# Token-wise softmax and logits turned by VectorE, and w1's split parts ordered behind h's

## The chip, the cores and the metric

The kernel runs on one core of one Trainium2 chip. The metric is device time of one execution in microseconds (us); the kernel before has 1101.79 us as the median of three runs (1101.53 to 1102.30). PE is the matrix engine, DVE the vector engine, ACT the scalar engine, POOL the general engine, SP the engine that issues most DMAs.

## What is computed

An attention over 8 batches with 32 state rows, then a dense expert over its 4608 tokens, then eight experts of which each token takes one:

```python
scores = scale * x @ state.T;   a  = softmax(scores)      # over the states
xread  = a @ state
scores2 = scale * state @ x.T;  a2 = softmax(scores2)     # over the 512 tokens
sread  = a2 @ x
x = concat([xread, sread], axis=2)                        # to 4608 rows of 512
h = x @ w_in;  x = (h * clip(h + 3, 0, 6) / 6) @ w_out
e_idx = argmax(x @ w_gate)                                # one expert for each token
h = maximum(x[mask] @ w1[e], 0);  ye = h @ w2[e]
out[mask] = gate_w * eom * ye
```

All matrices are float32. The large products are made of three: an operand is split into a high part and the rest, and high by high, low by high and high by low are added up.

## The kernel before

**Stages.** Each batch of 512 tokens is one segment of `segs`; two halves of batch 0 frame batch 1, batches 2 to 7 follow, and a last segment holds the 256 state rows. A segment goes through 16 f tiles of the dense expert. For each, `h_xread` makes h with six matmuls of 512 columns (L470), `act` makes g and its parts on ACT and DVE (L499 to L502: r, g, gh, gl), and `gemm2` adds twelve matmuls into four banks (L509 to L511), two tiles later (`LAG` is 2). At some f tiles work of other kinds is slipped in: `timetable` holds, by a step number, the attention of the next batch and the routing of the last one. The Tile scheduler orders each engine's instructions from this; each engine then works through its own list in order. A dependence of the kind `LATER` sets an order on one engine, or between two, and nothing else.

**The softmax over tokens.** `columns` leaves two tiles e (one for each half of the heads), 128 rows of head and state by 512 tokens, with their sums. For the read the tokens must lie on partitions: `cols_turn` (L361) transposes e in eight blocks on PE (L378), and ACT copies them from PSUM as `a2T` (L374). `cols_read` (L384) makes the read in 32 matmuls of 64 columns in four groups of partitions (L393), and ACT scales it by 1/sum (L399). `cols_x1` (L408) turns the 128x128 result with one more PE transpose (L421), which DVE splits as x1h and x1l (L418, L419). `x_loads` and `q_loads` fetch xT and xq, the batch's x in two layouts, through SP; the buffers of the next batch come free with the scores (L226) and the read (L393).

**Routing.** `routed` (L532) takes the dense output out of PSUM into the banks x2. `logits` (L564) makes four matmuls of 512 columns, one for each 128 features, into four groups of 32 partitions (L570). ACT copies the result as l (L575), `turn_logits` (L582) turns it on PE (L591), and DVE adds the four parts into `lg` (L588). `choose`, `ranks`, `place`, `sort_rows` and `scatter` work out each token's place. `write_rows` (L552) turns the rows with DVE (xr, L556) and has SP store them (xd, L562).

**Expert slots.** From about 690 us on 16 slots follow, each of up to 256 tokens of one expert by 8 f tiles, and some pairs. `gemm1` (L1028) makes the parts wh on ACT and wl on DVE of the f tile's w1 (L1034), 12 matmuls of 256 columns into h (L1038), the parts vh and vl of w2 (L1043, L1044), and takes h out of its bank as hh on ACT (L1047) and hl on DVE (L1048). `gemm2e` (L1053) comes two tiles later, `finish` scales the output (y, L1073), `turn` brings the next slot's rows (xt, L953; xh, xl, L973, L974).

Of the kernel before, what the change touches and what calls it, by code (L numbers as in the profile page):

```python
# [8 lines left out]
F32 = mybir.dt.float32  # L9
# [3 lines left out]
AF = mybir.ActivationFunctionType  # L13
# [33 lines left out]
def cat_consts():  # L47

    import numpy as np

    p = np.arange(128)[:, None]
    rows = {
        "desc": np.tile(np.arange(NE, 0, -1), 4),
        "base": np.arange(NE) * CAP,
        "eidx": np.tile(np.arange(NE), 2),
        "k256": np.arange(1, 18) * 256,
        "k256h": np.arange(18) * 256 + 129,
        "k64": np.arange(LEFT // 64 + 1) * 64,

        "pos1": np.array([s // 2 + (s % 2) * (N1 - N1 // 2) for s in range(N1)]),  # L60
        "posm": np.array([s // 2 + (s % 2) * (NM - NM // 2) for s in range(NM)]),
        "posu": np.arange(NU),
    }
    parts = {k: np.tile(np.asarray(a, np.float32), (128, 1)) for k, a in rows.items()}
    parts["half"] = p // 64
    parts["part64"] = p % 64
    parts["tri"] = p < np.arange(128)[None, :]
    off, n = {}, 0
    for k, a in parts.items():
        off[k] = (n, a.shape[1])  # L70
        n += a.shape[1]
    tok = np.zeros((128, NT // 128, 2), np.uint32)
    tok[:, :, 0] = np.arange(NT).reshape(-1, 128).T
    fill = np.zeros((NTAB, 2), np.uint32)
    fill[:, 0] = NT + np.arange(NTAB) % 128
    return off, np.concatenate(list(parts.values()), axis=1).astype(np.float32), tok, fill
# [3 lines left out]
def tile_kernel(  # L80
# [104 lines left out]
    def misc():  # L185
        users.append([])
        return psum("misc", 2), users[-1]
# [173 lines left out]
    def cols_turn(b):  # L361
# [19 lines left out]

        return part

    def cols_read(b):  # L384

        def part():
            a2, r2, copies = e2_t[b]
            x_q = [loads.pop((b, k, "q")) for k in range(2)]
            psR, done = misc()

            def mm(e, i, j):
                h = 2 * j + e
                return T.matmul(psR[32 * j:32 * j + 32, HD * e:HD * e + HD], a2[e][:, i, 32 * j:32 * j + 32],  # L393
                                x_q[h // 4][:, i, HD * (h % 4):HD * (h % 4) + HD], start=(i == 0), stop=(i == 3),
                                tile_position=(0, 32 * j))

            def use():
                for e in range(2):
                    done.append(S.activation(a2[0][:, 0, HD * e:HD * e + HD], psR[:, HD * e:HD * e + HD], AF.Copy,  # L399
                                             scale=r2[:, e:e + 1]).ins)  # L400
                e2_t[b] = a2[0][:, 0, :], list(done)

            return [lambda e=e, i=i, j=j: mm(e, i, j) for e in range(2) for i in range(4) for j in range(4)], \
                [*copies, *q_in[b]], use

        return part

    def cols_x1(b):  # L408

        def part():  # L410
            read, reads = e2_t.pop(b)
            psX, done = misc()
            psX = psX[:, :128]

            def use():
                hi, lo = [x[:, :, NS * b:NS * b + NS] for x in (x1h, x1l)]
                src = psX.rearrange("p (j s) -> p j s", j=4)
                done.append(V.tensor_copy(hi, src).ins)  # L418
                done.append(V.tensor_tensor(lo, src, hi.bitcast(F32), op=ALU.subtract).ins)  # L419

            return [lambda: T.transpose(psX, read, ident)], reads, use  # L421

        return part

    def attn_cols(b):

        if b < 2:
            columns(b, e2_t[b][0])
            yield
        one_run(cols_turn(b))  # L430
        yield
        one_run(cols_read(b))
        yield
        one_run(cols_x1(b))
        yield

    SW = {}
# [114 lines left out]
    def write_rows(r, c):  # L552

        xr = mp.tile([128, 8, 128], F32, tag="xr", name="xr", bufs=2)
        for k in range(4):
            i = V.transpose(xr[:, :, 32 * k:32 * k + 32], r.x2[k][:, 256 * c:256 * c + 256])  # L556
            for d in r.made[1::2]:
                tc.add_manual_dep(i.ins, d.name, LATER, reason="banks first")
        r0 = 128 * r.tile0 + 256 * c
        rows = xd[r0:r0 + 256, :].rearrange("(a u) (g n) -> g u a n", u=32, g=4)  # L560
        for g in range(4):
            D.dma_start(rows[g], xr[32 * g:32 * g + 32])  # L562

    def logits(r):  # L564

        def part():
            psl, done = misc()

            def mm(k):
                return T.matmul(psl[32 * k:32 * k + 32, :r.n], wg_sb[:, k, :], r.x2[k], start=True, stop=True,  # L570
                                tile_position=(0, 32 * k))

            def use():
                r.l4 = mp.tile([128, 512], F32, tag="r", name="l4")[:, :r.n]
                done.append(S.copy(r.l4, psl[:, :r.n]).ins)  # L575
                r.l4_made = done[-1]

            return [lambda k=k: mm(k) for k in range(4)], list(r.made), use

        return part  # L580

    def turn_logits(r):  # L582

        def part():
            pst, done = misc()

            def use():
                done.append(V.tensor_reduce(r.lg, pst[:, :r.n].rearrange("p (t k c) -> p t c k", t=r.nt, k=4),  # L588
                                            axis=AX.X, op=ALU.add).ins)

            return [lambda t=t: T.transpose(pst[:, 128 * t:128 * t + 128], r.l4[:, 128 * t:128 * t + 128], ident)  # L591
                    for t in range(r.nt)], [r.l4_made], use

        return part

# [100 lines left out]
    def route(r):  # L696

        at_will(logits(r))
        write_rows(r, 0)
        yield  # L700
        at_will(turn_logits(r))
        if r.n > 256:
            write_rows(r, 1)
        read_rows(r, 0)
        if r.n > 256:
            read_rows(r, 1)
        yield
        choose(r)
        ranks(r)
        yield  # L710
        place(r)
        sort_rows(r, 0, r.nt)
        if r.n > 256:
            return
        yield
        yield
        scatter(r, last_w[:1])
        yield
        yield
        zero_tails(0, 2)  # L720
        yield
        zero_tails(2, 4)
        yield
# [219 lines left out]
                apart(i, sooner, later_rows)  # L943
        return own

    got_first, last_turned, last_w = [], [], []

    def turn(xg, n):

# [78 lines left out]
    def gemm1(i, ft, xh, xl):  # L1028
# [3 lines left out]
        wh = mp.tile([128, 4, 128], R32, tag="gh", name="wh", bufs=3)  # L1032
        wl = mp.tile([128, 4, 128], R32, tag="gl", name="wl", bufs=3)
        last_w[:] = [S.copy(wh, a).ins, V.tensor_tensor(wl, a, wh.bitcast(F32), op=ALU.subtract).ins]  # L1034
        m = 0
        for w, x in ((wh, xh), (wh, xl), (wl, xh)):
            for k in range(4):
# [6 lines left out]
        V.tensor_tensor(vl, c, vh.bitcast(F32), op=ALU.subtract)  # L1044
        hh = qa["p"].tile([128, 256], R32, tag="hh", name="hh", bufs=3)
        hl = qa["p"].tile([128, 256], R32, tag="hl", name="hl", bufs=3)
        S.activation(hh, ps, AF.Relu)  # L1047
        i = V.scalar_tensor_tensor(hl, ps, 0.0, hh.bitcast(F32), op0=ALU.max, op1=ALU.subtract)  # L1048
        if ft == 6:
            tc.add_manual_dep(i.ins, last_turned[0].name, LATER, reason="the next rows first")  # L1050
        return ft, vh, vl, hh, hl
# [39 lines left out]
    def go(g, n=1):  # L1091
        return lambda: [next(g) for _ in range(n)]
# [72 lines left out]
    def X(b):  # L1165
# [12 lines left out]
        (1, 1): [I(9), go(cols[0]), lambda: q_loads(0)],  # L1178
        (1, 2): [I(10), go(cols[0])],
        (1, 3): [I(11), go(cols[0])],  # L1180
        (1, 4): [go(cols[0]), more_start, I(12)],
        (1, 5): [O(8), I(13)],
        (1, 6): [I(14), O(9)],
        (1, 7): [I(15), O(10)],
# [4 lines left out]
        (1, 12): [O(15), lambda: q_loads(1)],  # L1189
        (1, 13): [go(cols[1]), split_first],  # L1190
        (1, 14): [go(cols[1])],
        (1, 15): [go(cols[1], 2)],
        (0, 8): [load_part],
    }

# [4 lines left out]
    def timetable(b, r, att, shift):  # L1200
# [11 lines left out]
        for k in range(4, 10):  # L1212
            at(k, lambda: next(rows, None))
        if att:
            at(6, lambda: one_run(cols_turn(b)))
            at(7, lambda: one_run(cols_read(b), logits(r)))
            at(8, lambda: one_run(cols_x1(b), turn_logits(r)))
        else:
            at(6, lambda: one_run(logits(r)))
            at(7, lambda: one_run(turn_logits(r)))  # L1220
        at(9, lambda: choose(r))
        at(10, lambda: ranks(r))
        at(11, lambda: place(r), lambda: sort_rows(r, 0, 2))
# [4 lines left out]
    def half_timetable(b, r):  # L1228

        rows = attn_rows(b)  # L1230
        row = lambda: next(rows, None)
        return {
            2: [lambda: write_rows(r, 0)],
            3: [lambda: write_rows(r, 1), row],
            4: [lambda: one_run(logits(r)), row],
            5: [lambda: one_run(turn_logits(r)), lambda: choose(r), row, lambda: read_rows(r, 0), lambda: read_rows(r, 1)],
            6: [lambda: ranks(r), lambda: place(r), lambda: one_run(cols_turn(b)), row],
            7: [lambda: sort_rows(r, 0, 2), lambda: one_run(cols_read(b)), row, row, lambda: one_run(cols_x1(b))],
        }

    for n, (b, f0, f1) in enumerate(segs[:-1]):
# [221 lines left out]
```

## Time and profile before

| | before |
|---|---|
| median of three runs | 1101.79 us (1101.53 to 1102.30) |
| profiled execution | 1100.96 us, its span 1099.2 us |
| granted clock, mean | 0.999 of 2.4 GHz |
| PE busy | 1073.2 us (98%) |
| DVE busy | 714.5 us (65%) |
| ACT busy | 553.7 us (50%) |
| POOL busy | 126.2 us (11%) |
| DMA, mean rate | 134 GB/s |

The profiled execution is one of the kernel's executions, taken with a trace; the span is the time between its first and last recorded work. Busy is the union of an engine's instructions. Matmuls are pipelined, so that their records overlap, and where one begins says more than how long it is. A row with xN groups N like instructions that follow each other; its time runs from the first's start to the last's end.

### The profile page before, as it was taken

The page shows a single profiled execution, that of the slowest core. Times are in us where ns is not written, and L with a number is a line of the kernel's source. Part 1 is how long each engine was busy: PE and PEld are TensorE (multiplying, and loading weights), DVE is VectorE, ACT ScalarE, POOL GpSimd, SP SyncE. Part 2 cuts the span into 40 slices and gives each one's busy share as a digit, 9 for nine tenths or more (in the row PEclk, how much of TensorE's full clock was granted, in tenths as well). Part 3 has the DMA queues.
Part 4 walks back from the last instruction along what each step waited for, and adds up shares of the span by engine and source line. Part 5 has one row for each costly group of instructions (what it writes and reads, how often), then busy time and mean ns, then how long its engine had stood idle before and what let it go on. Part 6 is the DMA issues. An engine that isn't in the chain of part 4 may idle for free. (4 is left out here: it accounts for less than half of the span.)

```text
span 1099.2 us, 18698 instructions
## 1 busy us (share of the span) xinstructions
PE 1073.2 (98%) x6748; PEld 845.6 (77%) x6748; DVE 714.5 (65%) x1518; ACT 553.7 (50%) x1058; POOL 126.2 (11%) x138
## 2 busy tenths in 40 slices
PE   4999999999999999999999999999999999999997
PEld 1577777777777777777777899888869887988994
DVE  7988676755746747556554486986646655667761
ACT  4979644433433434334333344565545654566651
POOL 0000001230030030110300311220010010001001
PEclk9999999999999999999999999999999999999999
DMA  7657043613214114211130159676486679922500
GB/s 252 213 168 248 16 138 96 172 45 77 78 41 116 41 39 116 70 36 53 39 77 1 39 148 288 131 255 231 148 305 186 240 230 334 340 64 64 177 21 31
DMA packets 81251, 147.38 MB, mean 134 GB/s; under 512 B 13232, under 2 KB 49840, under 8 KB 81136
## 3 DMA queue, kind: packets, MB, share of 16 engines
q1 hardware_dynamic: 71776, 118.03, 34.7%
q0 software_dynamic: 9376, 28.09, 7.4%
q8 instruction: 55, 0.90, 0.4%
q14 instruction: 44, 0.36, 0.1%
HBM read 146.05 MB, written 29.68 MB: 160 GB/s over the span
## 5 line engine op out<-in xcount | busy, mean ns | idle before, releaser
L509 PE MATMUL o<-gh,wo 128*128 128x512 f32 x512 | 202.8, 396 | 0.0
L510 PE MATMUL o<-gh,wo 128*128 128x512 f32 x512 | 200.2, 391 | 0.2 <-DVE wo L782 0.2
L511 PE MATMUL o<-gl,wo 128*128 128x512 f32 x512 | 200.1, 391 | 0.0
L500 DVE SCALAR_TENSOR_TENSOR g<-r,h 128x512 f32<-128x512 f32 x128 | 87.3, 683 | 115.1 <-ACT r L499 114.6
L499 ACT ACTIVATE r<-h 128x512 f32<-128x512 f32 x128 | 76.4, 597 | 158.0 <-PE h L470 157.8
L1044 DVE TENSOR_TENSOR vl<-w2s,vh 128x512 fp32r<-128x512 f32 x128 | 87.8, 690 | 63.8 <-ACT vh L1043 56.2
L501 ACT CAST gh<-g 128x512 fp32r<-128x512 f32 x128 | 79.4, 620 | 82.2 <-DVE g L500 81.2
L1043 ACT CAST vh<-w2s 128x512 fp32r<-128x512 f32 x128 | 78.9, 621 | 78.7 <-PE o L1060 72.1
L502 DVE TENSOR_TENSOR gl<-g,gh 128x512 fp32r<-128x512 f32 x128 | 88.2, 689 | 44.7 <-ACT gh L501 39.3
L509 PEld LDWEIGHTS o<-gh,wo 128*128 128x128 f32 x512 | 96.1, 188 | 26.4 <-issue 6.1
L510 PEld LDWEIGHTS o<-gh,wo 128*128 128x128 f32 x512 | 96.2, 188 | 22.5 <-issue 1.5
L511 PEld LDWEIGHTS o<-gl,wo 128*128 128x128 f32 x512 | 96.1, 188 | 21.5 <-issue 1.0
L1034 DVE TENSOR_TENSOR wl<-w1s,wh 128x512 fp32r<-128x512 f32 x128 | 87.1, 688 | 35.2 <-ACT wh L1034 24.8
L1060 PE MATMUL o<-vh,hl 128*128 128x512 f32 x256 | 100.3, 392 | 0.9 <-DVE hl L1048 0.9
L1059 PE MATMUL o<-vl,hh 128*128 128x512 f32 x256 | 100.2, 392 | 0.0
L470 PE MATMUL h<-ah,sh 128*128 128x512 f32 x240 | 99.1, 414 | 0.9 <-ACT sh L453 0.7
L470 PE MATMUL h<-al,sh 128*128 128x512 f32 x240 | 94.7, 395 | 0.1
L470 PE MATMUL h<-ah,sl 128*128 128x512 f32 x240 | 93.8, 392 | 0.0
L1034 ACT CAST wh<-w1s 128x512 fp32r<-128x512 f32 x128 | 78.0, 621 | 29.5 <-PE h L1038 27.9
L1038 PEld LDWEIGHTS h<-xh,wh 128*128 128x128 f32 x512 | 76.9, 188 | 14.8 <-DVE hl L1048 2.4
L1038 PE MATMUL h<-xh,wh 128*128 128x256 f32 x512 | 82.1, 282 | 1.8 <-DVE hl L1048 1.8
L1056 PE MATMUL o<-vh,hh 128*128 128x512 f32 x256 | 81.2, 398 | 0.0
(234 smaller groups left out, 1770.8 us busy)
## 6 DMA issues: line engine op xcount, KB each, us to landing
w1s<-w SPq DMA_DIRECT2D x88, 512.0 KB
w2s<-w SPq DMA_DIRECT2D x88, 512.0 KB
xd<-xr SPq DMA_DIRECT2D x68, 128.0 KB
xt<-xd POOLq DMA_DIRECT2D x17, 512.0 KB
xT<-xT SPq DMA_DIRECT2D x16, 512.0 KB
wi<-w_in SPq DMA_DIRECT2D x16, 512.0 KB
wraw<-w_out SPq DMA_DIRECT2D x16, 512.0 KB
xq<-xq SPq DMA_DIRECT2D x16, 512.0 KB
```

Of the source, the lines that this page charges most:

```text
L470: T.matmul(ps, w[:, o:o + 128], a[:, e, :], start=(n == 0), stop=(n == 5))
L500: V.scalar_tensor_tensor(g6, r, 6.0, ps, op0=ALU.min, op1=ALU.mult)
L502: V.tensor_tensor(gl, g6, gh.bitcast(F32), op=ALU.subtract)
L509: T.matmul(po[k][:, :n], woh[ft][:, s], gh, start=first, stop=False)
L510: T.matmul(po[k][:, :n], wol[ft][:, s], gh, start=False, stop=False)
L511: T.matmul(po[k][:, :n], woh[ft][:, s], gl, start=False, stop=last)
L1034: last_w[:] = [S.copy(wh, a).ins, V.tensor_tensor(wl, a, wh.bitcast(F32), op=ALU.subtract).ins]
L1038: T.matmul(ps, w[:, k, :], x[:, k, :], start=(m == 0), stop=(m == 11))
L1044: V.tensor_tensor(vl, c, vh.bitcast(F32), op=ALU.subtract)
L1056: T.matmul(py[t], hh[:, sl], vh, start=(ft == 0), stop=False)
L1059: T.matmul(py[t], hh[:, sl], vl, start=False, stop=False)
L1060: T.matmul(py[t], hl[:, sl], vh, start=False, stop=(ft == 7))
```

## The change

Four things change.

1. *Softmax over tokens.* For batches 1 and 3 to 7 a new `cols_move` takes the place of `cols_turn`: DVE transposes each e within blocks of 32x32 into a tile `two`, and SP issues 16 DMAs, each of 32 partitions by 1 KB, that carry the blocks to their groups of partitions in `a2T`. Batches 0 and 2 stay with `cols_turn`. `cols_read` takes its weights from either layout. In `timetable` `cols_move` stands at step 5, the read at 7, where the turn stood at 6.
2. *State read.* In all batches `cols_x1` turns the result with DVE in place and with 16 DMAs of 32 partitions by 128 B; the split into x1h and x1l is now `cols_split`, one step later.
3. *Logits.* 16 matmuls of a quarter of the tokens each add up over the four feature blocks in PSUM, the four quarters in four groups of partitions, and DVE transposes the 128x128 result straight into `lg`. The copy l, `turn_logits` and the reduce go. Since a token now stands at another place of the tile, the table `tok` and the order in `write_rows` follow.
4. *Slots.* In `gemm1` wh and wl of f tiles 3 and 4 are ordered behind hh and hl of the tile two earlier.

```diff
+    def cols_move(b):
+
+        e2, s2, r2, _ = e2_t.pop(b)
+        V.tensor_scalar(s2, s2, 1e-9, None, op0=ALU.add)
+        V.reciprocal(r2, s2)
+        two, a2T = [ap.tile([128, 4, 2, 128], F32, tag="x4", name=n, bufs=4) for n in ("e2t", "a2T")]
+        moves = []
+        for e in range(2):
+            V.transpose(two[:, :, e].rearrange("p g (c n) -> p c g n", n=32),
+                        e2[e].rearrange("p (c g q) -> p c g q", g=4, q=32))
+        for j in range(4):
+            for g in range(4):
+                moves.append(D.dma_start(a2T[32 * g:32 * g + 32, j].rearrange("p e x -> p (e x)"),
+                                         two[32 * j:32 * j + 32, g].rearrange("p e x -> p (e x)")).ins)
+        e2_t[b] = [a2T[:, :, e] for e in range(2)], r2, moves
+        moved.append(b)
...
+            def w(e, i, j):
+                return a2[e][:, j, 32 * i:32 * i + 32] if b in moved else a2[e][:, i, 32 * j:32 * j + 32]
...
-                e2_t[b] = a2[0][:, 0, :], list(done)
+                e2_t[b] = a2[0]
...
     def cols_x1(b):
-        def part():
-            read, reads = e2_t.pop(b)
-            psX, done = misc()
-            psX = psX[:, :128]
-            def use():
-                hi, lo = [x[:, :, NS * b:NS * b + NS] for x in (x1h, x1l)]
-                src = psX.rearrange("p (j s) -> p j s", j=4)
-                done.append(V.tensor_copy(hi, src).ins)
-                done.append(V.tensor_tensor(lo, src, hi.bitcast(F32), op=ALU.subtract).ins)
-            return [lambda: T.transpose(psX, read, ident)], reads, use
-        return part
+        t = e2_t[b]
+        V.transpose(t[:, 1, :], t[:, 0, :])
+        for j in range(4):
+            for g in range(4):
+                D.dma_start(t[32 * g:32 * g + 32, 2, NS * j:NS * j + NS], t[32 * j:32 * j + 32, 1, NS * g:NS * g + NS])
+    def cols_split(b):
+        hi, lo = [x[:, :, NS * b:NS * b + NS] for x in (x1h, x1l)]
+        src = e2_t.pop(b)[:, 2, :].rearrange("p (j s) -> p j s", j=4)
+        V.tensor_copy(hi, src)
+        V.tensor_tensor(lo, src, hi.bitcast(F32), op=ALU.subtract)
...
     def attn_cols(b):
-        if b < 2:
-            columns(b, e2_t[b][0])
-            yield
-        one_run(cols_turn(b))
+        columns(b, e2_t[b][0])
+        if b:
+            cols_move(b)
+        yield
+        if not b:
+            one_run(cols_turn(b))
         yield
         one_run(cols_read(b))
         yield
-        one_run(cols_x1(b))
+        cols_x1(b)
+        yield
+        cols_split(b)
...
     def logits(r):
-            def mm(k):
-                return T.matmul(psl[32 * k:32 * k + 32, :r.n], wg_sb[:, k, :], r.x2[k], start=True, stop=True,
-                                tile_position=(0, 32 * k))
+            q = r.n // 4
+            def mm(k, j):
+                return T.matmul(psl[32 * j:32 * j + 32, :q], wg_sb[:, k, :], r.x2[k][:, q * j:q * j + q],
+                                start=(k == 0), stop=(k == 3), tile_position=(0, 32 * j))
             def use():
-                r.l4 = mp.tile([128, 512], F32, tag="r", name="l4")[:, :r.n]
-                done.append(S.copy(r.l4, psl[:, :r.n]).ins)
-                r.l4_made = done[-1]
-            return [lambda k=k: mm(k) for k in range(4)], list(r.made), use
-        return part
-    def turn_logits(r):
-        def part():
-            pst, done = misc()
-            def use():
-                done.append(V.tensor_reduce(r.lg, pst[:, :r.n].rearrange("p (t k c) -> p t c k", t=r.nt, k=4),
-                                            axis=AX.X, op=ALU.add).ins)
-            return [lambda t=t: T.transpose(pst[:, 128 * t:128 * t + 128], r.l4[:, 128 * t:128 * t + 128], ident)
-                    for t in range(r.nt)], [r.l4_made], use
+                done.append(V.transpose(r.lg.rearrange("p t c -> p (t c)"), psl[:, :q]).ins)
+            return [lambda k=k, j=j: mm(k, j) for k in range(4) for j in range(4)], list(r.made), use
...
+        if ft in (2, 3):
+            for i, d in zip(last_w, evicted[-2]):
+                tc.add_manual_dep(i, d.name, LATER, reason="h first")
...
-            at(6, lambda: one_run(cols_turn(b)))
+            at(5, lambda: cols_move(b))
             at(7, lambda: one_run(cols_read(b), logits(r)))
-            at(8, lambda: one_run(cols_x1(b), turn_logits(r)))
+            at(8, lambda: cols_x1(b))
+            at(9, lambda: cols_split(b))
         else:
             at(6, lambda: one_run(logits(r)))
...
```

How instructions move: on PE, in the dense stage of the batch whose attention is prepared near 360 us (b = 5), between the scores (L226) and the read there stood 32 regular matmuls and the turn (e is the softmax tile, ah, al, sh, sl are the parts of the h product):

```order
L509 MATMUL o_3366<-gh,wo_456 128x512
L510 MATMUL o_3366<-gh,wo_456 128x512
L511 MATMUL o_3366<-gl,wo_456 128x512
L470 MATMUL h<-ah_2982,sh_1_0_3330 128x512
L378 MATMUL misc<-ident,e_3475 128x128 x4
L378 MATMUL misc<-ident,e_3476 128x128 x4
L470 MATMUL h<-al_3021,sh_1_0_3330 128x512
L470 MATMUL h<-ah_2982,sl_1_0_3331 128x512
```

The same place now:

```order
L537 MATMUL o_3474<-gh,wo_456 128x512
L538 MATMUL o_3474<-gh,wo_456 128x512
L539 MATMUL o_3474<-gl,wo_456 128x512
L498 MATMUL h<-ah_3081,sh_1_0_3438 128x512
L498 MATMUL h<-al_3127,sh_1_0_3438 128x512
L498 MATMUL h<-ah_3081,sl_1_0_3439 128x512
```

The turn is gone, and 43 regular matmuls stand between the scores and the read instead of 32.

On SP, around the same batch, before (xd are stored rows, xT and xq the x of a later batch, st its state):

```order
L562 DMA xd<-xr 32x8x128 x8
L170 DMA xT_0_4079<-xT 128x1024
L170 DMA xT_1_4081<-xT 128x1024
L179 DMA xq_0_4128<-xq 128x1024
L179 DMA xq_1_4130<-xq 128x1024
L161 DMA st_4077<-sts 128x128
```

and now (L401 are the moves of the softmax, L440 those of the state read):

```order
L591 DMA xd<-xr 32x8x128 x8
L401 DMA a2T<-e2t 32x256 x16
L173 DMA xT_0_4213<-xT 128x1024
L173 DMA xT_1_4215<-xT 128x1024
L440 DMA a2T<-a2T 32x32 x16
L164 DMA st_4211<-sts 128x128
L182 DMA xq_0_4262<-xq 128x1024
L182 DMA xq_1_4264<-xq 128x1024
```

The 16 moves stand ahead of the next xT, and 16 more between that and st and xq.

On DVE, in the same batch, the split of the state read before (g and gl belong to the dense expert, lg and lmx to the routing):

```order
L500 SCALAR_TENSOR_TENSOR g_3658<-r,h 128x512
L502 TENSOR_TENSOR gl<-g_3658,gh 128x512
L418 CAST x1h<-misc 128x4x32
L419 TENSOR_TENSOR x1l<-misc,x1h 128x4x32
L588 TENSOR_REDUCE lg<-misc 128x128
L610 TENSOR_REDUCE lmx<-lg 128x4
```

and now, 15 rows behind the transpose of lg:

```order
L482 TENSOR_TENSOR sl_3_0_3869<-misc,sh_3_0_3868 128x512
L482 TENSOR_TENSOR sl_3_1_3871<-misc,sh_3_1_3870 128x512
L528 SCALAR_TENSOR_TENSOR g_3894<-r,h 128x512
L446 CAST x1h<-a2T 128x4x32
L447 TENSOR_TENSOR x1l<-a2T,x1h 128x4x32
L530 TENSOR_TENSOR gl<-g_3894,gh 128x512
```

The split stands behind all of `choose`, between a g and its gl.

On DVE at the first tiles of a slot (near 751 us in the trace) before:

```order
L1044 TENSOR_TENSOR vl<-w2s_5954,vh 128x512
L1048 SCALAR_TENSOR_TENSOR hl<-h,hh 128x256
L1034 TENSOR_TENSOR wl<-w1s_5955,wh 128x512 x2
L1034 TENSOR_TENSOR wl<-w1s_5956,wh 128x512 x2
L1048 SCALAR_TENSOR_TENSOR hl<-h,hh 128x256
L953 STREAM_TRANSPOSE xt<-xg 128x256 x3
L1048 SCALAR_TENSOR_TENSOR hl<-h,hh 128x256
```

and now:

```order
L1061 TENSOR_TENSOR vl<-w2s_6145,vh 128x512
L1065 SCALAR_TENSOR_TENSOR hl<-h,hh 128x256
L1048 TENSOR_TENSOR wl<-w1s_6146,wh 128x512 x2
L1065 SCALAR_TENSOR_TENSOR hl<-h,hh 128x256
L1048 TENSOR_TENSOR wl<-w1s_6147,wh 128x512
L1065 SCALAR_TENSOR_TENSOR hl<-h,hh 128x256
L1048 TENSOR_TENSOR wl<-w1s_6147,wh 128x512
```

Two of the four wl stand behind an hl each; the transposes of the next rows follow later.

## Rows read from the trace of the kernel before

**Rows 1.** The page's first part: busy us, share of the span, instructions.
```profile
PE 1073.2 (98%) x6748; PEld 845.6 (77%) x6748; DVE 714.5 (65%) x1518; ACT 553.7 (50%) x1058; POOL 126.2 (11%) x138
```

**Rows 2.** Windows: stretch, busy of PE, PEld, DVE, ACT, POOL; clock, DMA share, GB/s.
```profile
240.00:300.00 60.00, 60.00 (x376) 44.85 (x376) 37.14 (x70) 25.23 (x46) 5.75 (x6) 1.00 0.26 75
...
840.00:900.00 60.00, 59.39 (x381) 53.38 (x380) 39.50 (x77) 33.83 (x67) 3.98 (x4) 1.00 0.71 243
```

**Rows 3.** Timeline of PE, 284.6 to 297 us: start, duration, instruction, count.
```profile
284.87 0.39 PE L470 MATMUL h<-ah,sh 128*128 128x512 f32 x1
...
286.31 0.40 PE L470 MATMUL h<-ah,sl 128*128 128x512 f32 x1
...
287.01 0.39 PE L470 MATMUL h<-ah,sl 128*128 128x512 f32 x1
...
290.07 1.10 PE L393 MATMUL misc<-xq,a2T 128*32 128x64 f32 x64
290.99 0.60 PE L570 MATMUL misc<-x2T,wg_sb 128*32 128x512 f32 x2
...
291.96 0.50 PE L470 MATMUL h<-ah,sh 128*128 128x512 f32 x1
...
295.95 0.39 PE L511 MATMUL o<-gl,wo 128*128 128x512 f32 x1
...
296.96 0.39 PE L470 MATMUL h<-al,sh 128*128 128x512 f32 x1
```

**Rows 4.** What PE waited for: releaser, us in total, times, longest.
```profile
PE h L1038 <- DVE hl L1048: 1.8, 3, 0.6
...
PE h L470 <- ACT sh L453: 0.7, 1, 0.7
```

**Rows 5.** Timeline of PE at logits turned alone; a group: busy, mean ns, idle before.
```profile
591.12 0.39 PE L511 MATMUL o<-gl,wo 128*128 128x512 f32 x1
...
592.02 0.40 PE L470 MATMUL h<-al,sh 128*128 128x512 f32 x1
...
L378 PE MATMUL misc<-ident,e 128*128 128x128 f32 x56 | 7.5, 277 | 0.3 <-DVE sl L454 0.3
```

**Rows 6.** Timelines of ACT, DVE and PE at b=5; a group of DVE.
```profile
354.86 0.69 ACT L356 ACTIVATE e<-misc,sm 128x512 f32<-128x512 f32 x1
...
355.34 0.68 DVE L502 TENSOR_TENSOR gl<-g,gh 128x512 fp32r<-128x512 f32 x1
...
365.67 1.10 PE L393 MATMUL misc<-xq,a2T 128*32 128x64 f32 x64
...
378.36 1.29 DVE L454 TENSOR_TENSOR sl<-misc,sh 128x512 fp32r<-128x512 f32 x2 [1.38 <-ACT sh L453]
...
L307 DVE STREAM_TRANSPOSE bt<-misc 128x512 f32<-128x512 f32 x14 | 9.2, 696 | 5.5 <-PE misc L226 5.5
```

**Rows 7.** SP's DMA issues; DMA busy tenths in 40 slices of 180 to 190.
```profile
68.30 1.72 SPq L1137 DMA_DIRECT2D half<-xp  x2
...
182.08 1.34 SPq L562 DMA_DIRECT2D xd<-xr  x3
...
DMA  0000000000019999879700000799999989197899
```

**Rows 8.** Timelines of PE and DVE at the first tiles of a slot.
```profile
750.42 0.63 PE L1038 MATMUL h<-xh,wh 128*128 128x256 f32 x4
750.89 0.63 PE L1038 MATMUL h<-xl,wh 128*128 128x256 f32 x4
...
753.04 0.63 PE L1038 MATMUL h<-xh,wl 128*128 128x256 f32 x4
754.26 0.74 PE L1038 MATMUL h<-xh,wh 128*128 128x256 f32 x4 [0.59 <-DVE hl L1048]
...
751.97 1.90 DVE L1034 TENSOR_TENSOR wl<-w1s,wh 128x512 fp32r<-128x512 f32 x3 [2.48 <-ACT y L1073]
753.78 0.42 DVE L1048 SCALAR_TENSOR_TENSOR hl<-h,hh 128x256 fp32r<-128x256 f32 x1
```

More of the change, by code (lines that the diff above doesn't have):

```diff
@@ L72, in cat_consts @@
     tok = np.zeros((128, NT // 128, 2), np.uint32)
-    tok[:, :, 0] = np.arange(NT).reshape(-1, 128).T
+    for t0 in range(0, NT // 128, 4):
+        nt = min(4, NT // 128 - t0)
+        own = np.arange(128 * nt).reshape(4, nt, 32).transpose(0, 2, 1).reshape(128, nt)
+        tok[:, t0:t0 + nt, 0] = 128 * t0 + own
     fill = np.zeros((NTAB, 2), np.uint32)
@@ L382, in cols_turn @@
         return part
+    moved = []
+    def cols_move(b):
[13 more added lines that the diff above has]
+        moved.append(b)
     def cols_read(b):
@@ L392, in mm @@
                 h = 2 * j + e
-                return T.matmul(psR[32 * j:32 * j + 32, HD * e:HD * e + HD], a2[e][:, i, 32 * j:32 * j + 32],
+                return T.matmul(psR[32 * j:32 * j + 32, HD * e:HD * e + HD], w(e, i, j),
                                 x_q[h // 4][:, i, HD * (h % 4):HD * (h % 4) + HD], start=(i == 0), stop=(i == 3),
@@ L555, in write_rows @@
         for k in range(4):
-            i = V.transpose(xr[:, :, 32 * k:32 * k + 32], r.x2[k][:, 256 * c:256 * c + 256])
+            src = r.x2[k].rearrange("p (j m u) -> p m j u", j=4, u=32)[:, 2 * c:2 * c + 2]
+            i = V.transpose(xr.rearrange("p (m j) i -> p m j i", m=2)[:, :, :, 32 * k:32 * k + 32], src)
             for d in r.made[1::2]:
@@ L700, in route @@
         yield
-        at_will(turn_logits(r))
         if r.n > 256:
@@ L944, in load_own @@
         return own
-    got_first, last_turned, last_w = [], [], []
+    got_first, last_turned, last_w, evicted = [], [], [], []
     def turn(xg, n):
@@ L1046, in gemm1 @@
         hl = qa["p"].tile([128, 256], R32, tag="hl", name="hl", bufs=3)
-        S.activation(hh, ps, AF.Relu)
+        evicted.append([S.activation(hh, ps, AF.Relu).ins])
         i = V.scalar_tensor_tensor(hl, ps, 0.0, hh.bitcast(F32), op0=ALU.max, op1=ALU.subtract)
+        evicted[-1].append(i.ins)
         if ft == 6:
@@ L1180, in tile_kernel @@
         (1, 3): [I(11), go(cols[0])],
-        (1, 4): [go(cols[0]), more_start, I(12)],
+        (1, 4): [go(cols[0], 2), more_start, I(12)],
         (1, 5): [O(8), I(13)],
@@ L1191, in tile_kernel @@
         (1, 14): [go(cols[1])],
-        (1, 15): [go(cols[1], 2)],
+        (1, 15): [go(cols[1], 3)],
         (0, 8): [load_part],
@@ L1214, in timetable @@
         if att:
-            at(6, lambda: one_run(cols_turn(b)))
+            at(5, lambda: cols_move(b))
             at(7, lambda: one_run(cols_read(b), logits(r)))
-            at(8, lambda: one_run(cols_x1(b), turn_logits(r)))
+            at(8, lambda: cols_x1(b))
+            at(9, lambda: cols_split(b))
         else:
             at(6, lambda: one_run(logits(r)))
-            at(7, lambda: one_run(turn_logits(r)))
         at(9, lambda: choose(r))
@@ L1235, in half_timetable @@
             4: [lambda: one_run(logits(r)), row],
-            5: [lambda: one_run(turn_logits(r)), lambda: choose(r), row, lambda: read_rows(r, 0), lambda: read_rows(r, 1)],
+            5: [lambda: choose(r), row, lambda: read_rows(r, 0), lambda: read_rows(r, 1)],
             6: [lambda: ranks(r), lambda: place(r), lambda: one_run(cols_turn(b)), row],
-            7: [lambda: sort_rows(r, 0, 2), lambda: one_run(cols_read(b)), row, row, lambda: one_run(cols_x1(b))],
+            7: [lambda: sort_rows(r, 0, 2), lambda: one_run(cols_read(b)), row, row, lambda: cols_x1(b), lambda: cols_split(b)],
         }
```

## Prediction

> **What bounds the kernel now.** I read the page's first lines first: TensorE (PE) is busy 98% of the span, VectorE (DVE) 65%, ScalarE (ACT) 50% [rows 1]. Then a table by stretches: in 60 us of the dense stage PE is busy for all 60, and in the expert slots for 59.4, while DVE stands at 37 to 40 and the granted clock is 1.00, its upper level [rows 2]. Busy alone would not prove it, since ends of matmuls are modelled, so I read starts. In the timeline of PE, 128x512 matmuls begin 0.23 us apart without a gap (three spacings from 286.31 to 287.01) [rows 3]. So PE's own row of work is the bound from about 75 us on, and whatever leaves that row is worth its start-to-start time, as long as nothing new makes PE wait. Last I read who makes PE wait: after the first loads it is 1.8 us in three places of the slots and 0.7 us or less at single places [rows 4].
>
> **What leaves PE.** I price a block by the spacing of the regular matmuls around it, since entering and leaving a block of another shape costs too.
>
> *Second softmax turned by PE.* From 284.87 to 286.31 are two regular spacings (0.46) and the eight transposes: 1.44 - 0.46 = 0.98 us [rows 3]. Six of the eight batches lose this block: 5.9. At one of them PE also waited for 0.3 [rows 5]; that goes too: 6.2 in all. (The group counts 56 transposes; eight each of b=0 and b=2 stay.)
>
> *State read and logits turned by PE.* In five batches the two blocks, five transposes, stand together: 295.95 to 296.96 less 0.46 is 0.55 [rows 3], so 2.75. A block of four logit transposes alone is 591.12 to 592.02 less 0.46, 0.44 [rows 5], and there are three: 1.3. Five single transposes remain (three state reads, two for the last route of 256 rows); at an eighth of the 0.98 above they are 0.12 each: 0.6. Sum 4.65.
>
> *Logits.* Four matmuls of 512 columns become sixteen of 128. Before: 290.99 to 291.96, 0.97 us. The nearest row of small ones is the read itself, 32 matmuls of 64 columns, four groups of partitions at a time, in 290.07 to 290.99: eight rounds of 0.115 [rows 3]. By columns sixteen of 128 are four rounds of 0.23, 0.92; by count they are half the read, 0.46. If they did not run four at a time, each would cost between an eighth of the transposes, which go one after another, and a round of its own: 0.12 to 0.23, 2.0 to 3.7 in all. The read is the nearest row, so I take 0.92: 0.05 less in each of nine routes, 0.45; the bounds are -4.6 (by count) and +25 (one after another), the latter a rival below.
>
> What ACT and DVE lose or gain lies beside PE. ACT loses the copies out of PSUM. DVE gains per batch two transposes of 128x512 at 0.70, and two of 128x128, each at most as long; it loses a reduce over 512 columns and a copy, so at most +2.8 us [rows 6], in a batch of 75 us of which it idles more than a third [rows 2].
>
> One wait moves: once PE waited 0.7 for ACT's sh behind a block of scores [rows 4]. That block stands nine matmuls earlier now, so the wait may go, but a DVE instruction that waits for state-read moves stands close by. I take -0.35, bounds -0.7 and +1.
>
> **What the moves cost.** SP issues 16 DMAs for a turned softmax and 16 for a state read, one behind the other. *Does the read wait?* I follow b=5. The second exponential ends at 355.55 and DVE is free at 356.02; two small operations and two transposes at 0.70 end by 357.5 [rows 6]. Consecutive issues on SP are 0.45 apart where 128 KB leave SBUF (three in 1.34), and 0.86 for the two of half [rows 7]. The three issues that begin at 182.08 show traffic from 182.75 to about 185.0, so the last, begun at 182.97, landed within 2.05 [rows 7]. So the sixteenth move begins at 357.5 + 15 s and lands 2.05 later; with s = 0.45 that is 366.3. PE's read began at 365.67 [rows 6]; the turn before it is gone (-0.98), and it stands behind 11 more regular matmuls (+2.5): 367.2. The wait per batch is thus 15 s - 7.65: none at 0.45, none up to 0.51, 2.1 at 0.65. The margin is 0.9 us, so it is thin, but the places of b=1 and b=3 were put 10 and 11 matmuls later too. I take s = 0.45, the row of transfers out of SBUF, for which the wait is zero.
>
> The Trainium skill, "DMA: Bandwidth & Descriptors", section "Rules for kernel authors", says of many small transfers that they should be coalesced, and that under 64 KB one pays mostly overhead; the section "Anatomy of one DMA" gives a fixed 2.0 us for each on GpSimd's path. By that price, one at a time, 16 moves of 32 KB would take an estimated 33 us, not 9. The rows of SP speak for overlap: three began within 0.9 us and all had landed by 2.9 [rows 7].
>
> The Trainium skill, "VectorE: DVE Perf Modes", section "Rules for kernel authors", would leave a 128x128 transpose with TensorE if PSUM will do as its destination, and section "The three transpose paths" says that VectorE turns only 32x32 blocks. By that rule the turns would stay on PE and 10.85 of the sum below would not come. The trace bears out that PE turns a block quickly (0.12 each), but PE is the engine that is full here, which the rule does not weigh.
>
> *State read.* The read ends at 368.3, ACT scales it, and DVE turns it at about 369.3; the last of 16 moves lands at 369.3 + 15 x 0.45 + 2.05 = 378.1. cols_split stands on DVE between a g and its gl, two sl copies behind. In the trace before those sl copies end at 379.65 [rows 6], so DVE comes to it at about 380: almost 2 us of slack. If it waited, PE would feel it only behind two tiles of lag.
>
> *What is queued behind moves on SP.* xT and xq of the next batch, up to 15 us later, in stages where SP waited for PE anyway. Early on it is tighter: the moves of b=0 and b=1 push w_in, w_out and then xT of b=2 back by an estimated 7.2 us each (16 x 0.45). For all new waits together I take +1.2, bounds 0 and 4 (the thin margin of 0.9 overrun by 0.5 in each of six reads, and 1 us early).
>
> **Slots.** Three times PE waits 0.6 for hl [rows 4]. In one of them groups of four matmuls begin 0.47 apart (750.42, 750.89), so the group behind 753.04 was due at 753.51; it began at 754.26: 0.75 lost. It waited since the first f tile's h leaves its bank only with hl at 753.78, and DVE had wl of tiles 2, 3 and 4 ahead of that (751.97, three of them) [rows 8]. With wl of tile 3 behind hl of tile 1 and wl of tile 4 behind hl of tile 2, hl comes two wl (1.26) earlier and PE finds a free bank. That is 0.75 x 3 = 2.25. But the edges are order alone and every slot is ordered anew around them: ACT and DVE are busy 56% and 66% of the time there [rows 2], so new waits of 0.1 to 0.3 at a place are likely. So I take -1.9, with the full 2.25 as one bound and, as the other, a loss of 0.3 (half the wait that goes) in each of 16 slots, +4.8.
>
> **Sum.** -6.2 - 4.65 - 0.45 - 0.35 - 1.9 + 1.2 = -12.35. The profiled execution took 1100.96, of which 1099.2 is the span; it lies 0.8 under the median of 1101.79. Against its own time that is 1088.6, against the median 1089.4, which I give. About 0.2%, 2.2 us, is what a measurement of this kernel can tell from no change.
>
> **Rivals.**
> (B) *The moves land late.* With s at 0.60 to 0.66 each of six reads waits 1.4 to 2.3: 8 to 14 come back, 1097 to 1103. For it: 0.86 an issue occurs [rows 7]. Against: the transfers out of SBUF had 0.45. 0.12.
> (C) *The slots' new order makes new waits.* 0.3 us at a place in half to all of the 16 slots is 2.4 to 4.8 in place of -1.9: 1093.5 to 1096. For it: hl, vl, wl stand in one DVE queue. 0.10.
> (D) *SP is the new bound: slower.* At s = 0.86 a read waits 5.25, six times that 31.5: 1121. The point where it decides is s = 0.65, where 2.1 x 6 is all that was won; the place is the gap before each read. DMAs between partition groups within SBUF are not in the trace of before, so s is read from others. 0.10.
> (E) *The logits do not run four at a time.* At 0.23 each, +2.75 in each of nine routes: 1114. Against: the read does [rows 3]. 0.03.
> (F) *Every move pays its landing before the next begins.* 16 x 2.05 = 32.8 against 9.7: 23.1 us at each of six reads, 1228. Against: the overlap [rows 7]. The price of the Trainium skill, above, points this way. 0.02.
> (G) *More is won*: the logits go by count (-4.6) and no new wait comes (-1.2): 1084. 0.04.
>
> **How the numbers follow.** The forecast, 1085 to 1092, has 0.59. Faster by over 0.2%: 0.59 + 0.10 of C + 0.04 of G + 0.05 of B = 0.78; the same: 0.05 of B; slower: 0.10 of D + 0.03 of E + 0.02 of F + 0.02 of B = 0.17. The range 1084.5 to 1100 holds the forecast, C, over half of B and a part of G, about 0.78.
>
> **What would show it.** PE loses 90 transposes, and none stands between sh and al at b=4 to b=7. The last move before a read begins 7 us after the first. No idle time stands before the read's matmuls; if it does, its releaser is a DMA, and s says whether B or D. The four logit rounds last 0.9 behind the read. In the slots hl of the first tile comes ahead of the third wl, and h waits for hl no more. It would be wrong if DVE waited long at cols_split with g's partner behind it, or the wait before scores of b=2 were a DMA of xT.

## The result: slower, 1115.7 us

The changed kernel takes 1115.66 us (1115.33 to 1116.46, four runs) against 1101.66 of the kernel before on the same chip: a ratio of 1.0131, 95% interval 1.0116 to 1.0146. The prediction said 1089.4 and 1084.5 to 1100, so it was wrong in sign, and by 26 us. The profiled execution has a span of 1114.0 us, 14.8 more than before. Its page, to be read beside [rows 1] (the second row is the clock that was granted to PE in 40 slices):

```profile
PE 1069.4 (96%) x6874; PEld 848.1 (76%) x6874; DVE 718.3 (64%) x1538; ACT 544.5 (49%) x1037; POOL 125.0 (11%) x138
...
PEclk9999989999999999999999999999999999999999
```

PE is busy 3.8 us less than before, so work did leave it; but it is idle 18.6 us more. What it waits for (releaser, us in total, times, longest) answers [rows 4]:

```profile
PE misc L419 <- DMA a2T<-e2t: 15.0, 5, 6.3
...
PE misc L229 <- DMA xT<-xT: 3.4, 1, 3.4
PE misc L419 <- issue: 2.4, 1, 2.4
PE o L1078 <- DVE hl L1065: 0.8, 1, 0.8
```

All six reads that take moved blocks (L419 is the read's line now) wait for them, 17.4 us in all; the one marked "issue" stands behind its moves like the others. The scores of batch 2 (L229) wait for xT. The wait of h for hl in the slots, 1.8 us before, is gone.

Where PE's row stands tells where the time went. I compared the start of every 60th regular matmul in the two traces (times are those of the trace before). The changed kernel is 1.3 us behind at 125 us (most of it from the loads of the first 60 us; the version below that changes the slots alone shows 2.2 there), 14.2 behind at 157, 19.3 at 541, and 14.8 at the end. So 13 us are lost in one stretch of 32 us, another 5 in the five steady batches, and 4.5 come back from 600 us on.

**A steady batch.** SP's issues and PE near the read of b=5 in the changed kernel (start, duration, instruction; SP's first), beside [rows 6]:

```profile
374.85 10.24 SPq L401 DMA_DIRECT2D a2T<-e2t  x16
...
384.26 0.39 PE L538 MATMUL o<-gh,wo 128*128 128x512 f32 x1
386.76 1.10 PE L419 MATMUL misc<-xq,a2T 128*32 128x64 f32 x64 [2.11 <-DMA a2T<-e2t]
387.65 0.65 PE L601 MATMUL misc<-x2T,wg_sb 128*32 128x128 f32 x16
```

Sixteen moves fill SP for 10.2 us, 0.64 each. The last one begins 9.7 us after the first, and the read 2.2 us after that. The read was due at 384.5. While SP issues these moves, the 16 DMA engines are busy 0.19 of the time: they are far from full.

**The early stretch.** SP from 75 us on, then ACT's second exponential of batch 1, in the changed kernel:

```profile
82.45 10.54 SPq L440 DMA_DIRECT2D a2T<-a2T  x16
93.09 1.00 SPq L747 DMA_DIRECT2D wi<-w_in  x2
...
130.58 10.01 SPq L401 DMA_DIRECT2D a2T<-e2t  x16
142.07 2.49 SPq L1174 DMA_DIRECT2D part<-half  x2
145.20 11.40 SPq L440 DMA_DIRECT2D a2T<-a2T  x16
156.70 0.52 SPq L173 DMA_DIRECT2D xT<-xT  x1
...
128.92 0.72 ACT L359 ACTIVATE e<-e,sm 128x512 f32<-128x512 f32 x1 [0.44 <-DVE sm L358]
```

The same in the kernel before (a load of w_in, the exponential, xT of batch 2):

```profile
80.20 0.39 SPq L733 DMA_DIRECT2D wi<-w_in  x1
...
124.10 0.72 ACT L356 ACTIVATE e<-e,sm 128x512 f32<-128x512 f32 x1
...
134.39 0.80 SPq L170 DMA_DIRECT2D xT<-xT  x2
```

The moves of batch 0's state read hold back the loads of w_in and w_out by some 10 us, their conversion on ACT and DVE runs later, and the softmax of batch 1 with it. Then its moves take 10 us, the read waits 6.3, the state read's moves follow that, and xT of batch 2 is issued only behind them, at 156.70 instead of 134.39. PE and its clock in that stretch (windows: stretch, PE busy, granted clock, DMA share, GB/s):

```profile
142.29 1.93 PE L419 MATMUL misc<-xq,a2T 128*32 128x64 f32 x64 [6.31 <-DMA a2T<-e2t]
...
164.43 1.96 PE L229 MATMUL misc<-xT,st 64*32 64x512 f32 x16 [3.41 <-DMA xT<-xT]
...
143.00:146.00 3.00, 3.00 (x53) 0.51 0.69 208
146.00:149.00 3.00, 3.00 (x15) 1.00 0.45 153
...
166.00:169.00 3.00, 3.00 (x14) 0.50 0.47 96
```

Behind both waits PE runs at its lower level (1.2 GHz) for some 4 and 5 us, and 128x512 matmuls begin 0.43 apart instead of 0.23. So these waits cost more than their length.

### The profile page after: what moved, and what is told of

The parts are those of the page before. It is cut to its first block, busy times and chain, and to the rows that moved or that the text cites. A ratio compares the mean times of both kernels' runs of the same rounds, so it can differ in the third digit from the quotient of the medians.

```text
span 1114.0 us, 19264 instructions
## 1 busy us (share of the span) xinstructions
PE 1069.4 (96%) x6874; PEld 848.1 (76%) x6874; DVE 718.3 (64%) x1538; ACT 544.5 (49%) x1037; POOL 125.0 (11%) x138
## 5 line engine op out<-in xcount | busy, mean ns | idle before, releaser
L1055 PE MATMUL h<-xh,wl 128*128 128x256 f32 x512 | 81.3, 279 | 0.0
```

Source lines behind the costliest of these rows:

```text
L1055: T.matmul(ps, w[:, k, :], x[:, k, :], start=(m == 0), stop=(m == 11))
```

## The experiments

Theory 1: the parts that take work off PE are sound, and the DMAs between partition groups cost all the loss, through SP's time for each issue. Its rivals: the new order loses by itself; the moves are slow for landing or bytes, not for issues; the steady batches rather than the early stretch carry the loss. Ratios are to the kernel before on the same chip (1100.9 to 1101.5 us).

**No move at all.**

```diff
-            at(5, lambda: cols_move(b))
+            at(6, lambda: one_run(cols_turn(b)))
-            at(8, lambda: cols_x1(b))
-            at(9, lambda: cols_split(b))
+            at(8, lambda: one_run(cols_x1(b)))      # one PE transpose, as before
```

> The changed kernel without any move: the token-wise softmax and the state read are turned by PE as in the kernel before; the quarter-wise logits and the order in the slots stay. Theory 1 (the DMAs between partition groups cost all of the loss, the other two parts gain): PE keeps 56 + 8 transposes and loses 34; 5 x 0.44 + 3 x 0.45 + 0.2 for these, about 0.9 at the two late logits and 2.4 in the slots: about 1095 us, no wait for a DMA in the dense stage. Rival (the new order of the dense stage or of the slots loses by itself): 1102 or more.

Measured: 1093.2 us, ratio 0.9934 (0.9917 to 0.9950). The logits and the slots gain 7.7 us; theory 1 holds and its first rival falls. The trace is of the fastest of its four executions, with a span 9.1 us shorter than before. Its blocks, added up as the prediction did: five pairs of turns shrink from 0.56 to 0.13 (2.2), three blocks of four logit transposes go (1.4), two single ones (0.2), the two late logits, whose matmuls stand alone, cost 0.9 less, and a wait for sh before scores goes (0.8); with the slots below that is 8.1. The last 1.0 was not traced to single blocks.

**The state read turned by PE, the softmax by moves.** The same edit for `cols_x1` alone.

> The changed kernel with the state read turned by PE (one transpose), the softmax still by 16 moves a batch. Theory 1a (the second loss, 4.8 us before the scores of batch 2, comes from the 16 moves of the state read that stand ahead of xT on SP): that wait goes, eight transposes of 0.12 to 0.17 come back: about 1110 to 1112 us; the waits before the reads stay at 2 to 8 us. Rival (xT is late for another reason, or the waits before the reads only shift): 1114 or more.

Measured: 1103.5 us, ratio 1.0031 (1.0019 to 1.0042): 12 us better than the changed kernel, two to three times what I expected. The wait for xT went, as theory 1a says. What I had missed is the first group of moves: without those at 82 us, the exponential of batch 1 begins 3.5 us sooner, and its read waits 3.7 instead of 6.3. Between 125 and 157 us PE's row loses 4.3 us here, against 12.9 in the changed kernel.

```profile
125.45 0.72 ACT L359 ACTIVATE e<-e,sm 128x512 f32<-128x512 f32 x1
...
127.11 10.07 SPq L401 DMA_DIRECT2D a2T<-e2t  x16
138.67 2.31 SPq L1174 DMA_DIRECT2D part<-half  x2
141.03 2.20 SPq L173 DMA_DIRECT2D xT<-xT  x2
```

**The softmax turned by PE, the state read by moves.**

```diff
-            at(5, lambda: cols_move(b))
+            at(6, lambda: one_run(cols_turn(b)))
```

> The changed kernel with the softmax turned by PE in all batches, the state read still by 16 moves. Theory 1 (the moves of the softmax cost 22 us of waits before reads and delay all that stands behind them on SP): no wait before a read, xT of batch 2 some 10 us earlier and in time or nearly: 1094 to 1097 us. Rival (the moves of the state read alone cost several us through SP or DVE): 1100 or more.

Measured: 1095.9 us, ratio 0.9948 (0.9932 to 0.9965), as expected. Moving the state read saves PE 0.12 to 0.18 a batch and by the medians loses 2.7 us against the kernel without moves; the four times of each (1093.2 to 1097.8 here, 1092.1 to 1093.8 there) overlap, so this loss is not clear of the noise. In the profiled execution, the slowest of the four, all that it loses lies before 160 us, 1.5 us of it ahead of the first move: PE's turn of batch 1 waits 1.9 us, since the softmax is late, and with the lower clock behind that wait 3.6 us are lost there.

**Half of the softmax's moves.**

```diff
-        for j in range(4):
+        for j in range(2):
             for g in range(4):
                 moves.append(...)
-                return a2[e][:, j, 32 * i:32 * i + 32] if b in moved
+                return a2[e][:, j % 2, 32 * i:32 * i + 32] if b in moved
```

> The changed kernel with only 8 of the 16 moves of each turned softmax (the other half is left out, and the read takes the first half twice). Theory 1b (the wait before a read is the number of moves times SP's 0.63 us for each): the last move is issued 5 us earlier, the waits of batches 3 to 7 vanish and that of batch 1 falls from 7.7 to about 2.6: 1095 to 1100 us, with the wait for xT of batch 2 still there. Rival (the wait is landing time, or the softmax is late on ACT and DVE): the waits shrink by less than 1 us each, 1108 or more.

Measured: 1092.5 us, ratio 0.9930 (0.9913 to 0.9946), 23 us less than with all sixteen and a little below what I expected: the wait for xT of batch 2, which I thought would stay, went too. SP and PE at one read of a steady batch:

```profile
431.69 4.95 SPq L401 DMA_DIRECT2D a2T<-e2t  x8
...
438.61 0.39 PE L539 MATMUL o<-gl,wo 128*128 128x512 f32 x1
438.93 1.10 PE L419 MATMUL misc<-xq,a2T 128*32 128x64 f32 x64
439.84 0.62 PE L601 MATMUL misc<-x2T,wg_sb 128*32 128x128 f32 x16
```

Eight moves take 4.95 us, no steady read waits, and only batch 1 still does (3.5 us, since its read is due 3 us after its first move is issued). The wait goes with the number of moves. The bytes were halved with it, so this run alone does not tell issues from bytes; the next ones do, and so do the state read's moves, which carry 4 KB each and take as long as those of 32 KB.

**Two queues.** From here on the state read and batch 1 stay on PE, so that the steady batches are seen alone.

```diff
-                moves.append(D.dma_start(a2T...
+                moves.append((D, S)[g % 2].dma_start(a2T...
```

> State read turned by PE in all batches, the softmax of batches 0, 1 and 2 by PE too; batches 3 to 7 by the 16 moves, every second one issued on ACT's queue instead of SP's. Theory 1b (SP's 0.63 us for each of 16 issues makes the wait): with 8 issues on each queue the last lands about 7.5 us after the transposes, ahead of the read, so no wait is left: five turns of 0.99 less than the kernel without moves (1093.2), 1088 to 1090 us. Rival 1 (the transfers themselves, not the issues, take the time): waits of 2 us and more stay, 1098 or more. Rival 2 (5 us of issues a batch hold ACT's own work, and PE waits for r, gh or sh): 1093 or more.

Measured: 1092.9 us, ratio 0.9923 (0.9907 to 0.9940). Between the two: ACT and SP each issue a move in 0.64, side by side, four of the five reads wait 0.1 us or not at all, and one still waits 2.2, in the first of the batches (3), where the issues on both queues come 0.95 to 0.99 apart; why is not known. During the issues the DMA engines are busy 0.33 of the time, against 0.19 with one queue. So issues and not transfers take the time, and rival 1 falls. But hardly anything is won against the kernel without moves (1093.2; the intervals overlap), where 3 to 5 us were expected: 2.3 went at that read, 0.8 at the read of batch 2, and 1.5 between 632 and 765 us, in and behind the last logits. Why the slots lose there was not tried, and whether issues on ACT hold up other work (rival 2) stays open.

**POOL as the second queue.** `(D, G)[g % 2]`.

> As the version with two queues, but every second move is issued by POOL, which is busy 11% of the time, instead of ACT. Theory 1b: no wait if POOL needs less than about 0.9 us for an issue, 1088 to 1090 us. Rival (POOL needs 1 us and more for an issue, or its own work on the routing stands ahead): waits of 1 to 5 us before reads, 1092 to 1110.

Measured: 1092.6 us, ratio 0.9915 (0.9898 to 0.9932). POOL needs 0.50 for an issue, and the reads wait 0.9 once and 0.1 once. The same picture, with 2.2 lost between 632 and 765 us.

**Through DRAM.** One DMA out, four back.

```diff
-        for j in range(4):
-            for g in range(4):
-                moves.append(D.dma_start(a2T[32 * g:32 * g + 32, j], two[32 * j:32 * j + 32, g]))
+        D.dma_start(e2d[b], two)
+        for g in range(4):
+            moves.append(D.dma_start(a2T[32 * g:32 * g + 32], e2d[b].rearrange("(j i) g x -> g i j x", i=32)[g]))
```

> As these two, but the blocks go through DRAM: one DMA of 512 KB out and four of 128 KB back, all on SP. Theory 1b (the number of issues counts, not the bytes): five issues are some 2.5 us instead of 10, two landings of 2 to 2.4 us and two transfers of 512 KB (about 1.5 to 2.5 us each) follow each other: 8 to 10 us after the transposes, against some 10 that there are: waits of 0 to 1 us, 1088 to 1093 us. Rival (landing and bytes make the time): 2 us and more a read, 1098 or more.

Measured: 1089.4 us (1088.57 to 1089.97), ratio 0.9887 (0.9871 to 0.9904). This beats both kernels, and the one without moves too (its interval lies above this one). SP and PE in one batch:

```profile
428.45 0.34 SPq L400 DMA_DIRECT2D e2d<-e2t  x1
431.13 1.73 SPq L402 DMA_DIRECT2D a2T<-e2d  x4
432.90 0.43 SPq L174 DMA_DIRECT2D xT<-xT  x1
...
439.81 1.10 PE L420 MATMUL misc<-xq,a2T 128*32 128x64 f32 x64
```

The block of 512 KB goes out, and 2.7 us later its way back is issued; all five issues are done in 4.4 us. In the other batches that takes 4.4 to 5.1 us, and 7.5 in batch 3; no read of batches 3 to 7 waits. An issue from DRAM takes 0.42 with a spacing of 0.47, one from SBUF to SBUF 0.59 with 0.63.

**The slots' order alone,** in the kernel before.

```diff
+        if ft in (2, 3):
+            for i, d in zip(last_w, evicted[-2]):
+                tc.add_manual_dep(i, d.name, LATER, reason="h first")
```

> The kernel before with the order of wh and wl behind hh and hl in the slots alone. The rows of the changed kernel put the gain of this part at about 2.5 us (the lead of PE changes by 3.1 from 702 us on, some 0.6 of it at the last logits): 1098 to 1099 us. Rival (new waits elsewhere in the slots give it back): 1100 to 1102.

Measured: 1098.95 us, ratio 0.9973 (0.9963 to 0.9983). In the profiled executions PE's row gains 2.8 us from 648 us on. In the slots PE waits for hl only once, 0.2 us:

```profile
PE o L1064 <- DVE hl L1051: 0.2, 1, 0.2
```

**The steady batches' moves alone.** As with two queues, but all on SP.

> State read turned by PE in all batches, the softmax of batches 0 to 2 by PE, that of batches 3 to 7 by 16 moves on SP: the moves of the steady batches alone, beside the new logits and slots. Theory 1 with its two parts (the early part of the program, where the moves of batch 0 and 1 push loads and xT back, loses most; a steady batch loses 1 to 3 us at its read and wins 1): five reads that wait 1.7 to 2.9, 10 to 11 in all, less five turns of 0.99 against the kernel without moves (1093.2): 1098 to 1099 us. Rival (the steady batches carry the loss): 1103 or more, as the kernel with moves in batch 1 too.

Measured: 1100.7 us (1097.55 to 1102.79), ratio 0.9990 (0.9980 to 1.0001): between the theory (1098 to 1099) and its rival (1103). Moves in five steady batches cost 7.5 us against none, and the early stretch, with batch 1's moves and the state reads', the other 15 of the 22 that lie between no move and the changed kernel. The steady part is dearer than I wrote since some waits cost more than others:

```profile
293.12 1.10 PE L419 MATMUL misc<-xq,a2T 128*32 128x64 f32 x64 [1.97 <-issue]
...
445.74 1.76 PE L419 MATMUL misc<-xq,a2T 128*32 128x64 f32 x64 [2.25 <-DMA a2T<-e2t]
...
523.53 1.10 PE L419 MATMUL misc<-xq,a2T 128*32 128x64 f32 x64 [1.98 <-DMA a2T<-e2t]
...
293.00:296.00 3.00, 2.88 (x100) 1.00 0.58 179
...
447.00:450.00 3.00, 3.00 (x54) 0.60 0.78 255
...
525.00:528.00 3.00, 3.00 (x31) 0.52 0.02 5
```

Waits of 1.97 and 2.25 us are nearly alike, but behind the second one the granted clock is 0.60 and read and logits take 3.4 us instead of 1.9: 3.9 lost there, 2.1 at the first. The third is as long as the first, 1.98, and the clock falls behind it too, so the length of the wait alone does not decide. The times of this version scatter over 5 us, those of before over 2, and the granted clocks go with them: its mean is 0.999 in the three executions of 1097.6 to 1098.1 us and 0.994 in the one of 1102.8. At a clock of 0.999, then, the theory's 1098 to 1099 is met; what is beyond it goes with the clock. Why it falls behind one wait and not behind another was not shown.

## Why the prediction was wrong

*What bounds the kernel: right.* PE's row was the bound, and what left it without a new wait was won, as the kernel without moves shows (8.1 us by its blocks, 7.7 by the medians).

*What leaves PE: right in size.* Turns 6.2 forecast; the blocks of the trace before that are gone make 6.25. State read and logits turned by PE: 4.65 forecast, 4.9 measured. The logits: -0.05 a route forecast; sixteen matmuls cost 0.02 more than four, since from the start of the read to the next regular matmul it is 1.91 now and was 1.89 (rival E fell: they run four at a time). The late logits gave 0.9 instead of 0.1, and the wait for sh 0.8 instead of 0.35.

*What the moves cost: here it failed, at one number.* The formula, a wait of 15 s - 7.65 for a read, was near: with the measured 0.633 it gives 1.85, and the steady waits are 1.9 to 2.5. But I took s = 0.45, from three stores out of SBUF into DRAM [rows 7], and called them the nearest row. One by one they are:

```profile
182.08 0.33 SPq L562 DMA_DIRECT2D xd<-xr  x1
...
182.46 0.44 SPq L562 DMA_DIRECT2D xd<-xr  x1
...
182.95 0.47 SPq L562 DMA_DIRECT2D xd<-xr  x1
```

The first spacing is 0.38 and the second about 0.50; in most groups of four of these stores, too, the first spacing is short and the others are 0.49 to 0.52. So even this row, carried on to sixteen, stood at the end of the cover. A move from SBUF to SBUF takes 0.63. The range that I had written beside it (0.45 to 0.86) held the true value; with a margin of 0.9 us in 9.7, s = 0.51 was already the end of the cover, and the right conclusion from my own bounds was that a wait at the read was likelier than none. Rival B was priced right for the steady batches (1.4 to 2.3 a read) and had 0.12. Rival D had the right sign but not the cause: s stayed under its 0.65. With s = 0.633 the prediction's own sum gives about 1100.5; the other 15 us lie in the two terms that follow.

*What is queued behind the moves: failed in size.* I gave the early stretch 1 us in a bound of 4 for all new waits. It lost 13. Three things add up there. The moves of batch 0 hold up the weights' loads on SP, so that the softmax of batch 1 comes later (I had followed the loads to their own use, not to the ACT and DVE work that stands ahead of the softmax); 3.5 of the 4.8 us are theirs, as the version with the state read on PE shows, and by 1.3 PE's row was behind already. The read of batch 1 stands 10 matmuls, 2.3 us, later than before, against 12 us from the first move to the last landing; I had named that shift as a reason for its safety and not done the sum. And xT of batch 2 waits behind the state read's moves and is issued 22 us later than before, where I had 7.2 for each group; the wait of the scores for it is one of the signs that the prediction had named for being wrong. At `cols_split` I had almost 2 us of slack; in the changed kernel DVE waits there for the moves in seven batches, 14.6 us in all, and no wait of PE for it shows.

*What a wait costs: missing.* I priced each wait at its length. Behind some of them PE comes back at its lower clock, and the read, the logits and the next matmuls take up to twice as long: in b=4 a wait of 2.4 us cost 3.9. In the changed kernel that is so behind four of seven waits (6.3, 3.4, 2.2 and 2.4 us), and not behind those of 1.9, 2.1 and 2.5.

*Slots: right,* -1.9 forecast, 2.6 to 2.8 measured, above the bound of 2.25 that I had drawn from one gap. A fourth wait for hl, of 0.9 us, is in the trace before at another place of the slots, and I had left it out of the sum; with the slots' order alone it is down to the 0.2 shown above, in the changed kernel it is still 0.8.

The rule that moves should be few: the Trainium skill, "DMA: Bandwidth & Descriptors", section "Rules for kernel authors", wants many small transfers coalesced. I set it against rows of SP that overlap. Both are true. The moves do overlap, so the 2 us for each that its section "Anatomy of one DMA" gives for GpSimd's path are not paid one after another; but each has its 0.63 us on the queue, whether it carries 32 KB or 4 KB (16 of the latter take 10.5 to 11.4 us). Five large ones through DRAM took 4.4 us of SP and beat sixteen that go straight.

## What to carry to other kernels

A chain of small DMAs is priced as count times the queue's issue time, and that time is best read from DMAs with the same kinds of ends, in a long series and not from its first spacing; where no such row exists, the forecast goes by the point at which the cover is used up (here 0.51 of a possible 0.45 to 0.86), not by the cheapest row. Count what is queued behind the chain up to the last engine that needs it, where the program starts above all: here the early stretch lost 13 us, the five steady batches 5. When data must change partitions on a queue that also feeds the kernel, a few large transfers by way of DRAM can be cheaper than many within SBUF.

## What the hardware showed

An issue of 32 partitions between two places in SBUF took 0.59 to 0.60 us on SP and ACT (spacing 0.63 to 0.64) and 0.50 on POOL, one from DRAM to SBUF 0.42 on SP (spacing 0.47); 4 KB were no cheaper than 32 KB. That the kind of the ends makes the difference was not isolated. Waits of PE between 1.9 and 2.8 us left its clock at the upper level in some places (1.00 behind 1.97, 2.11 and 2.52 us, and behind 2.77 with the state read on PE) and not in others (it fell to the lower level behind 1.93 us with the softmax on PE, 1.98, 2.25 and 2.38); behind 3.4 and 6.3 us it was 0.50 and 0.51, for some 5 and 4 us.
